# Attention and gated experts in one kernel: two of the first tile's eight units turned on TensorE instead of VectorE, and the second expert matrix loaded six steps later

## The chip, the cores and the metric

The kernel runs on one core of one Trainium2 chip. The core has five engines that each work through their own list of instructions in order: TensorE (PE, matrix products; its weight loads are shown as PEld), VectorE (DVE), ScalarE (ACT), GpSimd (POOL) and SyncE (SP, which here only issues transfers). Products land in PSUM, which has eight banks; everything else lives in SBUF. The metric is the device time of one execution in microseconds (us). Before the change it is 502.42 us, the median of three runs (501.6 to 503.89).

## The reference

```
attn_out = softmax(q @ k.T / 8) @ v            # 8 batches, 16 heads, 384 tokens, 64 wide; k and v shared by the heads
x        = attn_out with the heads side by side  # 3072 tokens x 1024
g_logits = x @ w_group                         # 4 groups, the largest wins
e_logits = x @ w_expert[g]                     # 4 experts in the group, the largest wins
out      = gate(g) * gate(e) * (relu(x @ w1[g, e]) @ w2[g, e])
```

All inputs are float32. Each token goes to one of 16 experts, and each expert is two 1024 x 1024 matrices.

## The kernel before, in words

A batch of 384 tokens is cut into three tiles of 128 tokens, so there are 24 tiles (t) of the eight batches (b). A tile's 16 heads make eight units (u) of two heads each. The kernel is written out as 96 steps (i, in the loop over `NSL`), two units to a step, four steps to a tile, twelve to a batch. The order of the work is written by hand: each engine runs what the source emits in the order in which it is emitted. `at(step, place, fn)` puts a piece of work at a place inside a step, and `run(step, place)` emits it there.

One unit passes through these stations.

- `scores` (L211): four products on PE into a two-bank PSUM tile `s`, of which there are two. The next step's unit can only start when ACT has finished with the bank pair that it takes over.
- `soft` (L228, L233): one maximum over both heads on DVE, then two exponentials on ACT, which also write the row sums. The result is `pr`.
- `norm` (L244, L248): a reciprocal of the sums on DVE, then a multiplication of each head's `pr` on POOL, four for the two units of a step. `norm` of step 0 is put off into step 1, at place "b", which lies between the first unit's exponentials and the second unit's maximum; all others stand at the end of their own step.
- `transp` (L254): two steps later DVE turns each 32 x 32 block of `pr` into `ring`, a buffer with three groups of four units. The blocks are turned, but not moved, so a key's place is split over partitions and columns.
- `pv` (L272): in the last two steps of the following tile, PE multiplies the eight units of a tile with the values, in 96 products. Each uses 32 keys, both halves of the array's columns (one per head) and 256 columns (eight units of 32 tokens). Four PSUM banks take the sums of the four groups of partitions.
- `pv_out` (L286, L287): four ACT copies into `xt`, and one POOL copy to bfloat16 into `xb`.

After the first tile of a batch, `logits` (L295) forms the gate's products from `xt` alone, in step 8 of the batch: 32 products with the gate's weights held in the array and 32 tokens streamed each. `logits_out` (L305) turns the result on DVE, and `gate_first`, `gate_choose`, `gate_score` and `gate_pick` choose the expert that most tokens of the tile want. `load_main` (L469) then loads that expert's two matrices over POOL's queue, two transfers to a matrix. In batch 0 the first matrix is put in step 9 and the second in step 11; in the other batches both are in step 9.

From step 17 of a batch on, `main_expert` runs the batch's rows through this expert in pieces between the attention's own work (`advance`): first 64 products with the first matrix (L494), then the products with the second (L510). A last part, after step 95, handles the tokens that this leaves out.

PSUM has six tiles in all: two of `s`, and four single banks from `xbank` that all other products share in turn. `busy` (L99) is a product with no use for its result; one stands in step 2, one in step 3, one in step 9. Queries of the first tiles are turned on PE (`q_group`, L189), two heads to a turn, and copied out by ACT (L193). Transfers of q, k and v go through SP's queue in order. `load_v` repeats the values on four groups of 32 partitions, so that group a can be used with any block of 32 keys.

Of the kernel before, what the change touches and what calls it, by code (L numbers as in the profile page):

```python
# [9 lines left out]
FP32 = mybir.dt.float32  # L10
BF16 = mybir.dt.bfloat16
I32 = mybir.dt.int32
P = 128
# [6 lines left out]
def kernel(  # L20
# [11 lines left out]
    nc = tc.nc  # L32
# [53 lines left out]
    st = {}  # L86
# [2 lines left out]
    NB = S // 32  # L89

    TQ = 5

    def xbank():
        x = ps_x.tile([P, 512], FP32, tag="x", name="x")
# [69 lines left out]
    def load_v(b):  # L164

        v_sb = qpool.tile([P, NB, D], FP32, tag="v")
        vv = v[b, 0].rearrange("(r n) d -> r (n d)", n=NB)
        for i in range(P // 32):
            nc.sync.dma_start(out=v_sb[32 * i:32 * (i + 1), :, :].rearrange("r n d -> r (n d)"), in_=vv)
        st["v", b] = v_sb  # L170

    def scale_k(b):
        kk = st["kk", b]
# [68 lines left out]
    def norm(us):  # L242
        rinv = ppool.tile([P, 2, 2], FP32, tag="rinv")
        nc.vector.reciprocal(out=rinv[:], in_=st.pop(("ssum", us[0]))[:])  # L244
        for k, u in enumerate(us):
            for h in range(2):
# [2 lines left out]
                    out=pr, in0=pr, scalar1=rinv[:, k, h:h + 1], scalar2=1.0, op0=ALU.mult, op1=ALU.mult  # L249
                )  # L250

    def transp(u):

        nc.vector.transpose(  # L254
            out=ring[:, (u // 4) % 3, u % 4].rearrange("p h s -> p (h s)"),
            in_=st.pop(("pr", u))[:].rearrange("p h s -> p (h s)"),
        )

    def pv(t, n0, n1):

        v_sb = st["v", t // ST]
        a, z = sorted(((2 * t) % 3, (2 * t + 1) % 3))
        if n0 == 0:
            st["o", t] = [xbank() for _ in range(P // 32)]
        o = st["o", t]

        turned = lambda n, h: n - n % ST + (n + 1) % ST if t < ST and h else n
        for n in range(n0, n1):
            for i in range(P // 32):
                r = slice(32 * i, 32 * (i + 1))  # L270
                for h in range(2):
                    nc.tensor.matmul(  # L272
                        out=o[i][h * D:(h + 1) * D, 0:2 * P].rearrange("d (g c q) -> d g c q", g=2, c=4),
                        lhsT=v_sb[r, turned(n, h), :], rhs=ring[r, a:z + 1:z - a, :, h, ts(n, 32)],
                        start=(n == 0), stop=(n == NB - 1), tile_position=(32 * i, h * D),
                    )

    def pv_out(t):
        b, j = t // ST, t % ST
        if j < 2:  # L280
            st["xt", b, j] = pool.tile([P, KO, ST - 1 if j else 1, P], FP32, tag=f"xt{j}", name="xt", bufs=1)
        xt = st["xt", b, min(j, 1)][:, :, max(j - 1, 0), :]
        if j == 0:
            st["xb", b] = pool.tile([P, KO, S], BF16, tag="xb", name="xb", bufs=2)
        for i, o in enumerate(st.pop(("o", t))):
            nc.scalar.copy(out=xt[:, :, ts(i, 32)], in_=o[:, 0:2 * P].rearrange("p (c q) -> p c q", c=KO))  # L286
        nc.gpsimd.tensor_copy(out=st["xb", b][:, :, ts(j, P)], in_=xt)  # L287

    def logits(b, j0, j1):

        xt = st.pop(("xt", b, j0))
        lt_ps = xbank()
        for ko in range(KO):
            for c in range(4):
                nc.tensor.matmul(  # L295
                    out=lt_ps[ts(c, 32), 0:32 * (j1 - j0)].rearrange("e (j q) -> e j q", q=32),
                    lhsT=wge[:, ko, :], rhs=xt[:, ko, :, ts(c, 32)],
                    start=(ko == 0), stop=(ko == KO - 1), tile_position=(0, c * 32),
                )
# [187 lines left out]
    def expert(xb, w1, w2, result, psum, on_act=None, split=False):  # L487
# [3 lines left out]
        for fc in range(FO):  # L491
# [9 lines left out]
            else:  # L501
                nc.vector.tensor_scalar(out=h_t[:, fc, :], in0=hp[:, 0:S], scalar1=0.0, scalar2=None, op0=ALU.max)
            yield
        for j in range(ST):
            widths = (512, 256, 256) if split and j == ST - 1 else (512, 512)
            at_ = 0
# [45 lines left out]
        st["alone"].append(rows)  # L552

    def main_expert(b, on_act):
        w1, w2 = st.pop(("w", b))

        def store(j, done, y):
            if b < B - 1:
# [12 lines left out]
                ))  # L571

        result = scaled(lambda: st["gsel", b][0], store)
        yield from expert(st["xb", b], w1, w2, result, any_bank, on_act, split=(b == B - 1))

    def few_ready():

# [177 lines left out]


    NSL = NU // 2
    SB = ST * 4
    NT = B * ST
    pending = []  # L760
# [22 lines left out]
    for b in range(B):  # L783
# [65 lines left out]
    q_group(0, 0, 0, 1)  # L849
    q_group(0, 0, 1, 2)  # L850
    at(0, "b", q_group, 0, 0, 2, 4)
    at(1, "b", norm, (0, 1))
    load_v(0)
    for i in range(NSL):
        t, p = i // 4, i % 4
# [171 lines left out]
```

## Time and profile before

| | before |
|---|---|
| median of three runs | 502.42 us |
| profiled execution | 502.84 us |
| its span, first to last instruction | 501.4 us |
| PE busy | 479.0 us |
| DVE busy | 412.7 us |
| ACT busy | 319.7 us |
| POOL busy | 292.4 us |

In the rows of the profile a name such as `pr<-s,nmx` gives the tile written and the tiles read; `x48` is a count; a number in square brackets is how long the engine had been idle before, and what released it. A row of the timeline joins neighbouring instructions of one kind: its second number runs from the start of the first to the end of the last. A float32 product appears as two rows of PE, so the 48 products of half a `pv` are "x96".

### The profile page before, as it was taken

The page shows a single profiled execution, that of the slowest core. Times are in us where ns is not written, and L with a number is a line of the kernel's source. Part 1 is how long each engine was busy: PE and PEld are TensorE (multiplying, and loading weights), DVE is VectorE, ACT ScalarE, POOL GpSimd, SP SyncE. Part 2 cuts the span into 40 slices and gives each one's busy share as a digit, 9 for nine tenths or more (in the row PEclk, how much of TensorE's full clock was granted, in tenths as well). Part 3 has the DMA queues.
Part 4 walks back from the last instruction along what each step waited for, and adds up shares of the span by engine and source line. Part 5 has one row for each costly group of instructions (what it writes and reads, how often), then busy time and mean ns, then how long its engine had stood idle before and what let it go on. Part 6 is the DMA issues. An engine that isn't in the chain of part 4 may idle for free. (4 is left out here: it accounts for less than half of the span.)

```text
span 501.4 us, 20025 instructions
## 1 busy us (share of the span) xinstructions
PE 479.0 (96%) x8251; PEld 257.4 (51%) x8251; DVE 412.7 (82%) x744; ACT 319.7 (64%) x999; POOL 292.4 (58%) x532
## 2 busy tenths in 40 slices
PE   7798789999999999999999999999999999999992
PEld 2254445545555455555555455554555455555651
DVE  4989979988899889898799988998799888892450
ACT  5776866667666775766765865766667666662420
POOL 2665955684576654585476654684566754765232
PEclk9999999999999999999999999999999999999998
DMA  7703995399946998379965999379974996059994
GB/s 109 166 5 63 209 241 144 76 173 233 258 78 126 217 244 225 75 135 228 243 138 92 200 237 255 79 136 225 221 187 78 194 238 170 3 97 220 250 219 147
DMA packets 63388, 83.17 MB, mean 166 GB/s; under 512 B 20151, under 2 KB 39739, under 8 KB 63040
## 3 DMA queue, kind: packets, MB, share of 16 engines
q0 software_dynamic: 18736, 39.32, 42.3%
q1 hardware_dynamic: 43472, 42.22, 34.5%
q8 instruction: 66, 1.08, 0.9%
q10 hardware_dynamic: 1088, 0.33, 0.3%
q14 instruction: 26, 0.21, 0.1%
HBM read 101.52 MB, written 18.22 MB: 239 GB/s over the span
## 5 line engine op out<-in xcount | busy, mean ns | idle before, releaser
L233 ACT ACTIVATE pr<-s,nmx 128x384 f32<-128x384 f32 x384 | 217.7, 579 | 130.9 <-DVE nmx L228 116.7
L248 POOL TENSOR_SCALAR pr<-pr,rinv 128x384 f32<-128x384 f32 x384 | 217.3, 585 | 142.7 <-DVE rinv L244 129.5
L228 DVE TENSOR_REDUCE nmx<-s 128x2 f32<-128x768 f32 (+1 forms) x193 | 174.5, 944 | 47.6 <-PE s L211 46.5
L254 DVE STREAM_TRANSPOSE ring<-pr 128x768 f32<-128x768 f32 x192 | 175.3, 951 | 0.1
L211 PE MATMUL s<-kt,qt 64*64 64x384 f32 x1536 | 148.8, 497 | 10.8 <-ACT pr L233 8.7
L272 PE MATMUL x<-ring,v_sb 32*64 32x256 f32 x4608 | 137.6, 379 | 0.0
L272 PEld LDWEIGHTS x<-ring,v_sb 32*64 32x64 f32 x4608 | 101.6, 131 | 42.7 <-issue 23.0
L211 PEld LDWEIGHTS s<-kt,qt 64*64 64x64 f32 x1536 | 48.1, 132 | 78.8 <-ACT pr L233 38.6
L233 ACT ACTIVATION_READ_ACCUMULATOR pr<-s,nmx 128x1 f32 x384 | 77.8, 203 | 0.0
L494 PE MATMUL x<-xb,w 128*128 128x384 bf16 x448 | 76.6, 327 | 0.0
L494 PEld LDWEIGHTS <-w 128*128 128x128 bf16 x512 | 47.6, 97 | 42.3 <-issue 12.6
L510 PE MATMUL x<-w,h_t 128*128 128x512 bf16 x288 | 65.3, 380 | 0.0
L510 PEld LDWEIGHTS <-h_t 128*128 128x128 bf16 x392 | 36.3, 97 | 51.3 <-issue 12.1
L469 POOL DMA_DIRECT2D w<-in_moe_w_dram x36 | 27.5, 771 | 12.2 <-issue 7.4
L286 ACT COPY xt<-x 128x256 f32<-128x256 f32 x96 | 28.8, 387 | 2.9 <-PE x L272 2.9
L500 ACT ACTIVATE h_t<-x 128x384 bf16<-128x384 f32 x56 | 25.4, 502 | 6.1 <-PE x L494 6.1
L287 POOL CAST xb<-xt 128x1024 bf16<-128x1024 f32 x24 | 24.9, 1036 | 4.5 <-ACT xt L286 4.5
L529 ACT ACTIVATE y<-x,gsel 128x512 f32<-128x512 f32 x36 | 24.9, 692 | 3.4 <-PE x L510 3.4
L200 DVE STREAM_TRANSPOSE qt<-q_sb 128x512 f32<-128x512 f32 x38 | 26.1, 687 | 0.0
L510 PE MATMUL sb<-w,h_t 128*128 128x512 bf16 (+1 forms) x104 | 21.8, 363 | 0.0
L529 ACT ACTIVATE y<-sb,gsel 128x512 f32<-128x512 f32 (+1 forms) x10 | 6.7, 666 | 17.6 <-PE sb L510 15.2
L295 PEld LDWEIGHTS x<-xt,wge 128*32 128x32 f32 x1024 | 12.9, 110 | 5.8 <-ACT y L529 2.5
(136 smaller groups left out, 160.9 us busy)
## 6 DMA issues: line engine op xcount, KB each, us to landing
w<-in_moe_w_dram POOLq DMA_DIRECT2D x36, 1024.0 KB, 17.1
q_sb<-in_q_dram SPq DMA_DIRECT2D x76, 224.0 KB, 6.2
out_dram<-y SPq DMA_DIRECT2D x84, 128.0 KB, 6.7
xb_scratch<-xb SPq DMA_DIRECT2D x7, 768.0 KB, 4.3
v_sb<-in_v_dram SPq DMA_DIRECT2D x32, 96.0 KB, 3.6
kk<-in_k_dram SPq DMA_DIRECT2D x28, 92.0 KB, 3.5
q_sb<-in_q_dram SPq DMA_DIRECT2D x16, 128.0 KB, 3.4
q_sb<-in_q_dram ACTq DMA_DIRECT2D x2, 96.0 KB, 3.2
```

The costliest lines, as they stand in the source:

```text
L200: nc.vector.transpose(out=qt[:].rearrange("p (x d) -> p x d", d=32), in_=q_sb[:, :, 0:32])
L211: nc.tensor.matmul(out=s[m * D:(m + 1) * D, h, 0:S], lhsT=qt[r, ts(2 * cc + m, D)], rhs=kt[r, :], start=True, stop=True, tile_position=(h ...
L228: top = nc.vector.tensor_reduce(out=nmx[:, hs], in_=s[:, hs, 0:S], axis=AX.X, op=ALU.max, negate=True)
L233: ex = nc.scalar.activation(out=pr[:, h, :], in_=s[:, h, 0:S], func=ACTF.Exp, bias=nmx[:, h:h + 1], scale=1.0, accum_out=ssum[:, k, h:h + 1],)
L248: nc.gpsimd.tensor_scalar(out=pr, in0=pr, scalar1=rinv[:, k, h:h + 1], scalar2=1.0, op0=ALU.mult, op1=ALU.mult)
L254: nc.vector.transpose(out=ring[:, (u // 4) % 3, u % 4].rearrange("p h s -> p (h s)"), in_=st.pop(("pr", u))[:].rearrange("p h s -> p (h s)"),)
L272: nc.tensor.matmul(out=o[i][h * D:(h + 1) * D, 0:2 * P].rearrange("d (g c q) -> d g c q", g=2, c=4), lhsT=v_sb[r, turned(n, h), :], rhs=ri ...
L286: nc.scalar.copy(out=xt[:, :, ts(i, 32)], in_=o[:, 0:2 * P].rearrange("p (c q) -> p c q", c=KO))
L469: nc.gpsimd.dma_start(out=w[:, o:o + 4, :], in_=views[n][ds(e, 1), :, o:o + 4, :].rearrange("o p c f -> (o p) c f"))
L494: nc.tensor.matmul(out=hp[:, 0:S], lhsT=w1[:, ko, ts(fc, P)], rhs=xb[:, ko, :], start=(ko == 0), stop=(ko == KO - 1))
L510: nc.tensor.matmul(out=yp, lhsT=h_t[:, fo, ts(j, P)], rhs=w2[:, fo, at_:at_ + w], start=(fo == 0), stop=(fo == FO - 1),)
L529: nc.scalar.activation(out=y[:, at_:at_ + w], in_=yp, func=ACTF.Copy, scale=g)
```

## The change

Two of tile 0's eight units, units 1 and 3 (`WHOLE`), no longer go through `transp`. `whole` turns each of their heads on PE, three 128 x 128 turns into one bank, and ACT copies the bank into two places of `ring` that the first tile leaves free. These two units stand in steps 2 and 3, in place of the two products of `busy`.

A whole turn puts 128 keys on the partitions in one piece, so these units need the values in another layout. `v_whole` builds it in step 2 with twelve small POOL copies inside SBUF, into the space of `grem_all`, which is written for good only in step 18. `pv_whole` (steps 4 and 5) multiplies each of the two units with it, six products of 128 columns, into one bank, and `whole_out` (step 5) copies the result into `xt`.

The first tile's `pv` then has six units instead of eight: as many products as before, each over 192 columns instead of 256. Its `xt` holds the units in another order (0, 2, 4, 5, 6, 7, 1, 3), and the POOL copy to `xb` restores the right one in three pieces.

The gate's products of batch 0's first tile hold the tokens in the array and stream the gate's 32 columns: 8 products instead of 32, with the result already lying by tokens, so that `logits_out` becomes a plain DVE copy.

`norm` of steps 0, 2 and 3 (`LATE`) is put off into the following step's place "b"; before, only that of step 0 was. The second matrix of batch 0 is loaded in step 17 instead of step 11, and `expert` asks for it only when its second half begins. `scale_k` of batch 1 moves from step 7 to step 6. No other batch is touched.

```diff
+    WHOLE = (1, 3)
+    PARTS = [u for u in range(8) if u not in WHOLE]
+    order = PARTS + list(WHOLE)
+    slot_of = {u: x for x, u in enumerate(PARTS)}
...
+    def v_whole():
+        vw = grem_all[:].rearrange("p e j -> p (e j)").rearrange("p (h m d) -> p h m d", h=2, d=D)
+        for a in range(4):
+            r = slice(32 * a, 32 * (a + 1))
+            for h in range(2):
+                n = [keys(4 * m + a, h) for m in range(ST)]
+                for m0, m1 in ((0, ST),) if h == 0 else ((0, 2), (2, ST)):
...
+                    nc.gpsimd.tensor_copy(out=vw[r, h, m0:m1, :], in_=st["v", 0][r, n[m0]:end:step, :])
...
+    def whole(u):
+        pr = st.pop(("pr", u))
+        prt = ring[:, 1, 2 + WHOLE.index(u)]
+        for h in range(2):
+            pt = xbank()
+            for m in range(ST):
+                nc.tensor.transpose(out=pt[:, ts(m, P)], in_=pr[:, h, ts(m, P)], identity=ident[:])
+            nc.scalar.copy(out=prt[:, h, :], in_=pt[:, 0:S])
+
+    def pv_whole(u):
...
+        for m in range(ST):
+            for h in range(2):
+                nc.tensor.matmul(
+                    out=st["ow"][h * D:(h + 1) * D, ts(k, P)], lhsT=st["vw"][:, h, m, :],
+                    rhs=ring[:, 1, 2 + k, h, ts(m, P)], start=(m == 0), stop=(m == ST - 1), tile_position=(0, h * D),
+                )
...
     def transp(u):
+        if u in slot_of:
+            nc.vector.transpose(
+                out=ring[:, slot_of[u] // 4, slot_of[u] % 4].rearrange("p h s -> p (h s)"),
...
+            return
+        if u in WHOLE:
+            return
...
+        nc_ = len(PARTS) if t == 0 else 8
...
+                    to = o[i][h * D:(h + 1) * D, 0:32 * nc_]
...
+            if b == 0 and j0 == 0:
+                nc.tensor.matmul(
+                    out=lt_ps[:, 0:32], lhsT=xt[:, ko, 0, :], rhs=wge[:, order[ko], :],
+                    start=(ko == 0), stop=(ko == KO - 1),
+                )
+                continue
...
-        nc.vector.transpose(
+        (nc.vector.tensor_copy if b == 0 and j0 == 0 else nc.vector.transpose)(
...
+    LATE = (0, 2, 3)
...
-            at(s0 + (9 if b else 11), "g", load_main, b, 1)
+            at(s0 + (9 if b else 17), "g", load_main, b, 1)
...
-            at(s0 + 7, "g", scale_k, b + 1)
+            at(s0 + (7 if b else 6), "g", scale_k, b + 1)
...
-    for x, where in ((2, "m2"), (3, "m2"), (9, "m3")):
-        at(x, where, busy, ident)
+    for x, u in enumerate(WHOLE):
+        at(2 + x, "m2", whole, u)
+        at(4 + x, "m2", pv_whole, u)
+    at(5, "e", whole_out)
+    at(2, "g", v_whole)
+    at(9, "m3", busy, ident)
...
-        if i:
+        if i in LATE:
+            at(i + 1, "b", norm, us)
+        else:
             norm(us)
```

More of the change, by code (lines that the diff above doesn't have):

```diff
@@ L170, in load_v @@
         st["v", b] = v_sb
+    def v_whole():
[5 more added lines that the diff above has]
+                for m0, m1 in ((0, ST),) if h == 0 else ((0, 2), (2, ST)):
+                    step = n[m0 + 1] - n[m0] if m1 - m0 > 1 else 1
+                    end = n[m1 - 1] + (1 if step > 0 else -1)
+                    nc.gpsimd.tensor_copy(out=vw[r, h, m0:m1, :], in_=st["v", 0][r, n[m0]:end:step, :])
+        st["vw"] = vw
     def scale_k(b):
@@ L250, in norm, with keys, whole_out, first_xt @@
                 )
-    def transp(u):
+    def keys(n, h):
+        return n - n % ST + (n + 1) % ST if h else n
+    def whole(u):
[7 more added lines that the diff above has]
+    def pv_whole(u):
+        k = WHOLE.index(u)
+        if k == 0:
+            st["ow"] = xbank()
+        for m in range(ST):
[4 more added lines that the diff above has]
+                )
+    def whole_out():
+        nc.scalar.copy(
+            out=first_xt()[:, len(PARTS):KO, :], in_=st.pop("ow")[:, 0:2 * P].rearrange("p (c q) -> p c q", c=2)
+        )
+    def first_xt():
+        if ("xt", 0, 0) not in st:
+            st["xt", 0, 0] = pool.tile([P, KO, 1, P], FP32, tag="xt0", name="xt", bufs=1)
+        return st["xt", 0, 0][:, :, 0, :]
+    def transp(u):
+        if u in slot_of:
+            nc.vector.transpose(
+                out=ring[:, slot_of[u] // 4, slot_of[u] % 4].rearrange("p h s -> p (h s)"),
+                in_=st.pop(("pr", u))[:].rearrange("p h s -> p (h s)"),
+            )
+            return
+        if u in WHOLE:
+            return
         nc.vector.transpose(
@@ L285, in pv_out @@
         for i, o in enumerate(st.pop(("o", t))):
-            nc.scalar.copy(out=xt[:, :, ts(i, 32)], in_=o[:, 0:2 * P].rearrange("p (c q) -> p c q", c=KO))
-        nc.gpsimd.tensor_copy(out=st["xb", b][:, :, ts(j, P)], in_=xt)
+            nc.scalar.copy(
+                out=xt[:, 0:nc_, ts(i, 32)], in_=o[:, 0:32 * nc_].rearrange("p (c q) -> p c q", c=nc_)
+            )
+        if t == 0:
+            for at0, at1 in ((0, 2), (2, 6), (6, 8)):
+                c0, c1 = order[at0], order[at0 + 1]
+                nc.gpsimd.tensor_copy(
+                    out=st["xb", b][:, c0:order[at1 - 1] + 1:c1 - c0, ts(j, P)], in_=xt[:, at0:at1, :]
+                )
+        else:
+            nc.gpsimd.tensor_copy(out=st["xb", b][:, :, ts(j, P)], in_=xt)
     def logits(b, j0, j1):
```

24 lines of the change are left out of this document (17 added, 7 removed).

## The prediction

> **What bounds the kernel now.** I read the page's busy shares first, then a table of stretches, then the timeline of the first 110 us, where all edits lie. The first fence has the page's shares and the stretches, whose columns are the stretch, its length, the busy time of PE, PEld, DVE, ACT and POOL with counts, the granted clock, the DMA share and GB/s.
>
> ```profile
> PE 479.0 (96%) x8251; PEld 257.4 (51%) x8251; DVE 412.7 (82%) x744; ACT 319.7 (64%) x999; POOL 292.4 (58%) x532
> ...
> 15.00:20.00 5.00, 3.75 (x30) 0.98 (x32) 5.00 (x8) 3.63 (x14) 2.65 (x5) 1.00 1.05 205
> 20.00:25.00 5.00, 3.74 (x32) 1.40 (x32) 5.00 (x9) 3.25 (x10) 3.53 (x7) 1.00 0.50 104
> 30.00:35.00 5.00, 5.00 (x140) 3.00 (x128) 4.18 (x6) 2.89 (x11) 2.26 (x4) 1.00 0.02 7
> ...
> 56.00:74.00 18.00, 15.14 (x336) 8.11 (x336) 15.29 (x24) 12.35 (x41) 11.79 (x20) 1.00 1.11 223
> 81.00:98.00 17.00, 17.00 (x325) 9.58 (x313) 15.89 (x32) 11.88 (x39) 9.60 (x19) 1.00 0.36 70
> ...
> 100.00:400.00 300.00, 300.00 (x5266) 161.16 (x5251) 264.62 (x443) 203.83 (x644) 185.18 (x322) 1.00 0.83 178
> ```
>
> From some 75 us on PE never rests, and nothing edited there is PE work. Before that DVE is full (15 to 25 us) or PE (30 to 35 us). So whatever an edit saves or costs before 75 us moves all that follows by the same amount, and the question is what each early step gains.
>
> **Steps 2 to 5: DVE, and behind it a loop.** The timeline gives start, duration, engine and line.
>
> ```profile
> 12.95 1.83 DVE L228 TENSOR_REDUCE nmx<-s 128x2 f32<-128x768 f32 x2
> 14.69 1.83 DVE L254 STREAM_TRANSPOSE ring<-pr 128x768 f32<-128x768 f32 x2
> 15.04 0.58 ACT L233 ACTIVATE pr<-s,nmx 128x384 f32<-128x384 f32 x1
> 16.06 0.21 ACT L233 ACTIVATION_READ_ACCUMULATOR pr<-s,nmx 128x1 f32 x1
> 16.32 0.88 PE L211 MATMUL s<-kt,qt 64*64 64x384 f32 x8 [0.25 <-ACT pr L233]
> 16.44 0.14 DVE L244 RECIPROCAL rinv<-ssum 128x4 f32<-128x4 f32 x1
> 16.50 1.79 DVE L228 TENSOR_REDUCE nmx<-s 128x2 f32<-128x768 f32 x2
> 27.08 1.81 DVE L228 TENSOR_REDUCE nmx<-s 128x2 f32<-128x768 f32 x2
> ```
>
> A maximum takes 0.87 us of DVE (two from 12.95 to 14.69), a turn 0.875 (14.69 to 16.44), a reciprocal 0.06 until the next starts (16.44 to 16.50). Two, two and one make 3.55 per step; the first maxima of steps 2 and 6 stand at 12.95 and 27.08, 14.13 apart, which is four such steps.
>
> Take a turn away, and another limit is near. A unit's two exponentials hold its `s` for 1.23 us (15.04 to 16.27), its successor's scores start 0.05 later and take 0.88, the maximum starts 0.06 after that and needs 0.96, the exponential starts 0.03 later: 3.21 us per step, whatever DVE has to do. So two turns (1.75 us) can't be won whole.
>
> I now go through the new order with these durations. Step 2: two maxima and one turn, 2.6 us of DVE, so the loop decides: step 3's first maximum at 16.14 instead of 16.50. Step 3 has 2.7 us of DVE, so the loop again: step 4's first maximum at 19.35. Step 4 has two turns and two reciprocals (3's was put off into it); its second maximum waits for the second unit's loop until 20.48, then 0.87 + 1.75 + 0.06 lead to 23.16. Step 5 is unchanged, 3.55: step 6 begins at 26.71 instead of 27.08. **Gain 0.37 us.** What is late next is the ACT-to-scores loop, not DVE.
>
> **What this leans on.** POOL, PE and ACT must keep up in these steps.
>
> ```profile
> 10.46 1.97 SPq L169 DMA_DIRECT2D v_sb<-in_v_dram  x4
> DMA to landing us min/median/max: 2.5/2.9/3.1
> 13.13 2.26 POOL L248 TENSOR_SCALAR pr<-pr,rinv 128x384 f32<-128x384 f32 x4 [0.25 <-DVE rinv L244]
> L436 POOL TENSOR_TENSOR gw<-wt 128x12 f32<-128x12 f32 x8 | 1.7, 208 | 6.8 <-DVE wt L433 6.8
> L603 POOL CAST c<-ident 128x128 bf16<-128x128 f32 x1 | 0.3, 293 | 0.0
> L248 POOL TENSOR_SCALAR pr<-pr,rinv 128x384 f32<-128x384 f32 x384 | 217.3, 585 | 142.7 <-DVE rinv L244 129.5 <-DVE es L431 13.0
> 6.89 0.87 PE L189 MATMUL x<-ident,q_sb 128*128 128x128 f32 x6
> 13.68 1.13 PE L99 MATMUL x<-ident 128*128 128x512 f32 x2
> ```
>
> `v_whole`: twelve copies of 64 to 192 columns. No such copy is in the trace; the nearest rows are 208 ns (12 columns), 293 ns (128) and 585 ns (384), so the twelve cost 2.5 to 7.0 us; I take 0.29 each, 3.5 us, since 128 columns is their mean. The values have landed before 15.6 (last issue before 12.43, at most 3.1 more). The copies stand behind `norm` of step 1 (until 15.39) and end near 18.9; behind them `norm` of step 2 ends at 21.2. Its first unit is then ready at 20.05 and the second at 21.2; DVE asks for them at 21.35 and 22.2. Cost nothing, but with little to spare: at 0.585 each the copies end at 22.4, the first turn waits until 23.5 and the second until 24.7 instead of 22.2, and up to 2.5 us are lost.
>
> `whole`: six turns take 0.87 us, where `busy` took 1.13; PE waits for ACT there, so nothing. Its two ACT copies stand between the exponentials of one step and the next, in the 1.25 us that ACT spent waiting there; two of 384 columns take some 0.8. `pv_whole` (two times 12 rows) lies in PE's waits in steps 4 and 5, and `whole_out`, one more copy of 256 columns, in ACT's wait in step 5. All four cost nothing while the loop's 3.21 stands; without that cover each would cost its 0.4 to 0.9 once.
>
> **Steps 6 and 7: PE.**
>
> ```profile
> 27.80 2.85 PE L272 MATMUL x<-ring,v_sb 32*64 32x256 f32 x96
> 30.57 1.52 PE L211 MATMUL s<-kt,qt 64*64 64x384 f32 x16
> 31.52 1.82 DVE L228 TENSOR_REDUCE nmx<-s 128x2 f32<-128x768 f32 x2 [0.82 <-PE s L211]
> 32.02 2.85 PE L272 MATMUL x<-ring,v_sb 32*64 32x256 f32 x96
> 35.74 1.82 DVE L228 TENSOR_REDUCE nmx<-s 128x2 f32<-128x768 f32 x2 [0.60 <-PE s L211]
> 36.84 0.76 PE L295 MATMUL x<-xt,wge 128*32 128x32 f32 x64
> 38.08 0.88 PE L211 MATMUL s<-kt,qt 64*64 64x384 f32 x8 [0.48 <-ACT pr L233]
> 39.90 1.78 DVE L228 TENSOR_REDUCE nmx<-s 128x2 f32<-128x768 f32 x2
> ```
>
> The next scores queue behind `pv`, and DVE waits for them, 0.82 and 0.60 us. The 96 rows follow each other at 26 ns; streaming 192 columns instead of 256 would make it 19.6 ns, and a half 2.2 us, 0.65 less. The ends are 0 (the rows don't stream-bind) and 0.65 to 0.7 (DVE's own chain, 34.05 against 35.74, allows no more). I take 0.65 and 0.63: that rows can follow faster shows in the gate's products, 64 rows of 32 columns in 0.76 us. **Gain 1.28 us.**
>
> **Step 8, the gate.** Eight products with the tokens held. Each of its 16 rows loads 128 x 128 in float32; the turns do that at 0.105 us a row (0.87 for six), which makes up to 1.9 us against 0.76. PE has 0.48 to spare before the next scores, and their maximum at 39.90 starts 0.94 after the scores end at 38.96. 1.2 us more just fits under 1.36. Cost nothing; between a gain of nothing and a loss of 0.3. The DVE copy in place of a turn of 32 columns, three POOL copies for one, and `scale_k` a step earlier on a POOL that is 58% busy: nothing, POOL's rows lie two steps ahead of their use.
>
> **The second matrix.**
>
> ```profile
> 55.94 1.55 POOL L469 DMA_DIRECT2D w<-in_moe_w_dram  x2
> 65.49 0.88 PE L211 MATMUL s<-kt,qt 64*64 64x384 f32 x8 [1.15 <-DVE nmx L228]
> 82.95 2.26 POOL L248 TENSOR_SCALAR pr<-pr,rinv 128x384 f32<-128x384 f32 x4 [1.95 <-DVE es L431]
> 106.98 3.63 PE L510 MATMUL x<-w,h_t 128*128 128x512 bf16 x16
> ```
>
> Its two issues leave POOL at 55.94 and come back in the 1.95 us that POOL waits ahead of 82.95: nothing. The transfer took 18 us there (55.94 to 74, DMA share 1.11) and moves to some 81 to 98, where the share is 0.36. SP's loads of queries, issued shortly before and behind it, will take longer; the matrix is first used at 106.98, so it has 8 us to spare. At 65.49 a unit's scores came 1.15 us late, although `s` was free; the weight loads there name "issue". It is the only gap of that kind in the run, and lies in the stretch that the second matrix fills. Ends: nothing, and 1.15 gained. The trace doesn't show the cause, and 98 to 128 us is as full without such a gap, so I take the middle, **0.6 us.**
>
> **Sum.** 0.37 + 1.28 + 0.6 = 2.25 us off the profiled execution's 502.84, which is its span of 501.4 and 1.4 around it: 500.6. The median shown lies 0.42 lower, so 500.2 against 502.42.
>
> **The rivals.**
> - *Narrower products are no shorter.* Then 0.37 + 0.6: 501.4. For it: a half's weight loads span almost as long as its products. Against it: the gate's 64 rows in 0.76 us. The Trainium skill, "TensorE: Matmul & The Clock Gate", section "Wait — 56ns, not 53.3ns?", gives a floor of about 25 ns from one small product to the next, "however small N is"; by that a half would fall by only 0.1. The gate's rows, 12 ns apart, disagree, though each product makes two of them.
> - *GpSimd is late.* At 0.585 us per copy `v_whole` loses 2.5 and leaves 2.25 - 2.5: 502.7. Against it: POOL's small rows near 0.29.
> - *TensorE's clock falls, and the kernel is slower.* `busy` goes from steps 2 and 3. These rows, with PE's busy time, clock, DMA share and GB/s, show that the clock can halve.
>
> ```profile
> 18.81:22.33 3.52, 2.34 (x20) 1.00 0.28 61
> 492.00:494.00 2.00, 0.47 (x20) 1.00 0.74 285
> 498.00:500.00 2.00, 0.00 (x0) 0.50 0.01 4
> ```
>
> At half speed scores last 0.88 longer in each of steps 2 to 5 and each half of `pv` 2.2: 3.5 + 4.4 more, some 508. It decides if the clock falls for as little as 3 us. Against it: 18.81 to 22.33 has no `busy`, PE is two thirds full there, and the clock is 1.00; it fell only some 4 us after all PE work had ended. The Trainium skill, same page, "Part 4: PE-mode transpose", says that transposes don't count as PE-busy "the same way", which speaks for this rival; the two steps from 18.81 to 25.9, with turns and scores alone, don't bear it out.
> - *The gap at 65.49 stays, or another comes where the matrix now loads:* 0.6 to 1.7 less, 500.8 to 501.9.
>
> **How the numbers follow.** Forecast 0.47, with its own range 499.3 to 500.9; products no shorter 0.20; the gap stays or moves 0.16; GpSimd late 0.11; clock 0.06. The best sum, with all of the gap, is 2.8 off 502.42: 499.6, less 0.4 for the scatter of medians. The upper end takes in the late copies, 502.7. So 499.2 to 502.8. One measurement of this kernel tells about 0.5%, 2.5 us, from no change: the forecast lies just inside. Faster by more (under 499.9) 0.40, mostly the forecast with all of the gap; within 0.45; slower 0.15, the clock and late copies together with a moved gap.
>
> **What would show it.** Step 6's first maximum near 26.7, step 8's near 34.1 (from the profile's start); a half of the first `pv` at 2.2 us; twelve copies near 0.29 on POOL; PE's clock 1.00 throughout; no wait of DVE for POOL at its turns in step 4; no gap before scores between 60 and 100 us. Wrong if the first `pv` keeps 2.85, if turns in step 4 wait for `norm`, or if the loop takes more than 3.3 us per step.

## The result and the profile after

| | before | after |
|---|---|---|
| median of 17 runs each | 502.23 us | 500.77 us |
| range of these runs | 500.96 to 505.87 | 498.84 to 502.46 |
| span of the profiled execution | 501.4 us | 498.9 us |

The ratio is 0.9959, with a 95% interval of 0.9941 to 0.9976. The medians lie 1.46 us apart, and the interval allows 1.2 to 3.0. With another 12 runs of the changed kernel the ratio was 0.9967 (0.9948 to 0.9986). So the gain is real, some 0.3 to 0.4%, and smaller than the half per cent that the prediction counted as a difference.

The page's shares after, and of the stretches that the prediction showed of before these:

```profile
PE 479.3 (96%) x8218; PEld 262.1 (53%) x8235; DVE 411.5 (82%) x742; ACT 321.0 (64%) x1004; POOL 295.6 (59%) x546
...
15.00:20.00 5.00, 3.79 (x34) 1.47 (x38) 4.12 (x6) 4.82 (x18) 4.76 (x16) 1.00 1.12 214
...
56.00:74.00 18.00, 16.30 (x342) 9.08 (x342) 16.41 (x28) 13.80 (x47) 11.41 (x21) 1.00 0.63 153
81.00:98.00 17.00, 17.00 (x345) 10.19 (x345) 16.14 (x30) 12.03 (x40) 11.53 (x23) 1.00 0.90 173
100.00:400.00 300.00, 299.42 (x5193) 162.29 (x5191) 264.19 (x442) 204.45 (x646) 182.21 (x318) 1.00 0.84 179
```

From 15 to 20 us DVE is no longer full (4.12 of 5), ACT almost is (4.82), and POOL went from 2.65 to 4.76. The granted clock is 1.00 in every stretch. The second matrix's transfer left 56 to 74 us (DMA share 1.11 before, 0.63 now) and came to 81 to 98 (0.36, now 0.90). In the last row PE is 0.58 us short of full, where before it was full. These are eleven pieces of 0.05 us; a second profile of the same code, with 17 more records of PE, has none of them, so they are records that this one lacks and not rests.

The timeline of the first 40 us and of step 15, after:

```profile
15.37 3.17 POOL L185 COPY grem_all<-v_sb 32x192 f32<-32x192 f32 x12
16.18 0.96 DVE L244 TENSOR_REDUCE nmx<-s 128x2 f32<-128x768 f32 x1 [0.48 <-PE s L227]
19.47 0.96 DVE L244 TENSOR_REDUCE nmx<-s 128x2 f32<-128x768 f32 x1 [0.32 <-PE s L227]
21.46 1.83 DVE L304 STREAM_TRANSPOSE ring<-pr 128x768 f32<-128x768 f32 x2
26.78 1.82 DVE L244 TENSOR_REDUCE nmx<-s 128x2 f32<-128x768 f32 x2
27.50 2.21 PE L335 MATMUL x<-ring,v_sb 32*64 32x192 f32 x96
34.17 1.82 DVE L244 TENSOR_REDUCE nmx<-s 128x2 f32<-128x768 f32 x2
35.35 1.87 PE L371 MATMUL x<-wge,xt 128*128 128x32 f32 x16
...
61.87 1.52 PE L227 MATMUL s<-kt,qt 64*64 64x384 f32 x16
63.32 2.85 PE L335 MATMUL x<-ring,v_sb 32*64 32x256 f32 x96
```

The maxima at 16.18 and 19.47 now wait for PE's scores: DVE has time to spare. The first half of `pv` takes 2.21 us. The maximum of step 8 starts at 34.17, where it started at 35.74. In step 15 the two units' scores run in one row of 16, 1.52 us, and `pv` follows at once; the pause of 1.15 us between the two units' scores at 65.49 is gone.

In what follows, a step's start is the start of the first `nmx` row on DVE that belongs to it (16.18, 19.47, 26.78 and 34.17 above are steps 3, 4, 6 and 8), and its length is the distance to the next step's start. Steps of one kind have the same length in most places (4.22 or 4.23 us for the ones with half a `pv`), so a longer one stands out. Worked out this way, after minus before:

| start of step | 3 | 4 | 6 | 7 | 8 | 15 | 16 | 48 | 60 | 72 | 95 |
|---|---|---|---|---|---|---|---|---|---|---|---|
| us | -0.32 | -0.54 | -0.30 | -0.93 | -1.57 | -1.59 | -2.97 | -3.48 | -2.78 | -2.20 | -2.11 |

So 1.57 us is won by step 8, another 1.38 in step 15 (5.61 to 4.23 us long), and some 0.5 more by step 48. Then 1.4 us is lost, in steps that no edit touches: step 55 is 4.83 instead of 4.23, step 63 is 4.47, step 67 is 4.56. This is what the prediction did not have, and what most of the experiments are about.

### The profile page after: what moved, and what is told of

It is laid out like the page before. It is cut to its first block, busy times and chain, and to the rows that moved or that the text cites. A ratio compares the mean times of both kernels' runs of the same rounds, so it can differ in the third digit from the quotient of the medians.

```text
span 498.9 us, 19995 instructions
## 1 busy us (share of the span) xinstructions
PE 479.3 (96%) x8218; PEld 262.1 (53%) x8235; DVE 411.5 (82%) x742; ACT 321.0 (64%) x1004; POOL 295.6 (59%) x546
## 5 line engine op out<-in xcount | busy, mean ns | idle before, releaser
L311 DVE STREAM_TRANSPOSE ring<-pr 128x768 f32<-128x768 f32 x184 | 168.1, 952 | 0.1
L335 PE MATMUL x<-ring,v_sb 32*64 32x256 f32 (+1 forms) x4608 | 137.2, 376 | 0.1
L335 PEld LDWEIGHTS x<-ring,v_sb 32*64 32x64 f32 x4608 | 103.0, 131 | 41.1 <-issue 23.1
L353 ACT COPY xt<-x 128x256 f32<-128x256 f32 (+1 forms) x96 | 28.6, 386 | 2.5 <-PE x L335 2.5
L363 POOL CAST xb<-xt 128x1024 bf16<-128x1024 f32 x23 | 23.8, 1036 | 4.5 <-ACT xt L353 4.5
L429 POOL TENSOR_TENSOR mask_all<-oh 128x48 bf16<-128x48 f32 x8 | 2.1, 269 | 22.4 <-DVE oh L425 22.4
```

The lines of the kernel that those rows point to most:

```text
L311: nc.vector.transpose(out=ring[:, (u // 4) % 3, u % 4].rearrange("p h s -> p (h s)"), in_=st.pop(("pr", u))[:].rearrange("p h s -> p (h s)"),)
L335: nc.tensor.matmul(out=to.rearrange("d (c q) -> d c q", c=nc_) if t == 0 else to.rearrange("d (g c q) -> d g c q", g=2, c=4), lhsT=v_sb[r, ...
L353: nc.scalar.copy(out=xt[:, 0:nc_, ts(i, 32)], in_=o[:, 0:32 * nc_].rearrange("p (c q) -> p c q", c=nc_))
```

## The experiments

Each is the changed kernel with one edit, unless another is named. Where no number of runs is given, the time is that of one execution, and the kernel before stood at 502.18 to 502.32 us beside it. Single executions of one kernel scatter by some 2 us either way, once by 3.6 (the two ranges above), so these experiments are read by the lengths of their steps, not by their totals.

### The transfer of the second matrix, put back or moved alone

```diff
-            at(s0 + (9 if b else 17), "g", load_main, b, 1)
+            at(s0 + (9 if b else 11), "g", load_main, b, 1)
```

> The changed kernel, with the second matrix loaded in step 11 again. Theory A (the transfer of the second matrix made the gap of step 15): step 15 is 5.4 to 5.6 us long again, and everything behind it 1.2 to 1.4 us later than in the changed kernel. Theory B (the gap hangs on where the blocks of PE's instruction list end, and the change has moved these ends by some 32 instructions): step 15 stays at 4.2 us.

The kernel before with only this line the other way round, and the second matrix asked for when it is first used:

> The kernel before, with the second matrix in step 17 and nothing else. PE's list of instructions is the same as before. Theory A: step 15 falls from 5.6 to 4.2 us. Theory B: step 15 stays at 5.2 to 5.6 us, since the block ends at the same place.

Measured: 502.38 us with the transfer put back, 500.95 us with the transfer moved alone. The first starts 1.5 us late (its step 2 starts at 14.49 instead of 12.98, which no edit explains). Step 15 is 4.26 and 4.24 us long, so the gap is gone in both. PE's timeline with the transfer put back:

```profile
69.70 0.52 PE L377 MATMUL x<-xt,wge 128*32 128x64 f32 x18
71.22 0.87 PE L377 MATMUL x<-xt,wge 128*32 128x64 f32 x46 [1.00 <-issue]
```

The gap has moved into step 16, between two of the gate's products, with no releaser but "issue". So each theory is borne out by one run and missed by the other. The gap at 65.49 went with the transfer, but the transfer doesn't say where a gap falls; nor does a gap in step 15 need it, since two kernels below, the one without turns and the one with 192 more instructions, load the second matrix in step 17 too, and their step 15 is 5.76 us long. What differs ahead of step 15 between the kernel before and this one is the number of PE's instructions: the first tile's edits take some 32 away by step 8.

The DMA view shows what comes late. Packets, megabytes and share of the engines by queue, from 60.5 to 62.5 and from 62.5 to 64.5 us, first in the kernel before, then with the transfer moved alone:

```profile
q0 software_dynamic: 178, 0.36, 95.7%
q1 hardware_dynamic: 79, 0.07, 13.3%
...
q0 software_dynamic: 153, 0.31, 82.8%
q1 hardware_dynamic: 153, 0.14, 26.4%
q8 instruction: 1, 0.02, 2.9%
```

and

```profile
q1 hardware_dynamic: 476, 0.40, 110.6%
q8 instruction: 1, 0.02, 4.2%
...
q1 hardware_dynamic: 309, 0.44, 108.7%
```

q8 is the queue that loads instructions: 66 packets of some 16 KB in a run. These two kernels have the same PE list up to there. With the matrix (q0) on the engines, the packet comes only in the later stretch, and the gap at 65.49 opens behind it.

### Sixteen products without a use at PE's start

`busy` behind the first one gets sixteen more products of 16 columns, whose results are not used. The trace counts two PE instructions for each, 32 in all.

```diff
+        for _ in range(more):
+            nc.tensor.matmul(out=x[:, 0:16], lhsT=a[:], rhs=a[:, 0:16], start=True, stop=True)
...
-    busy(ones)
+    busy(ones, 16)
```

> The changed kernel with 16 tiny products more (32 PE instructions) behind the very first product, where PE waits for the first transfer of k. Theory B: the blocks end at the places of the kernel before, so the long steps are those of before (15, 31 and 43) and not those of the changed kernel (43, 55, 63 and 67); up to step 14 nothing changes by more than 0.1 us. Theory A: the steps' lengths stay those of the changed kernel.

Measured: 499.97 us. The steps begin 0.28 us later (step 2 at 13.26 instead of 12.98), and yet the last one starts 0.75 us earlier than in the changed kernel (443.64 against 444.39). Step 43 is 4.23 us long instead of 4.56, step 63 4.23 instead of 4.47, step 67 4.23 instead of 4.56; step 79 is longer (4.45 against 4.28), and step 55 stays long (4.60 against 4.83). Neither theory has this list right: steps 15 and 31, which were to be long again, are 4.26 and 4.23. How much of it is the padding's own shows in the second profiles further down. Steps 43 and 79 are alike in both profiles of the changed kernel (4.56 and 4.57; 4.28 and 4.23) and in both versions padded by 32 (4.23 and 4.23; 4.45 and 4.45). Steps 55, 63 and 67 are 4.28, 4.23 and 4.23 in the changed kernel's second profile, with nothing added. So 32 more instructions at the start move what is lost in these two steps, 180 and 350 us later; the other three can be the one execution.

### The whole turns taken out

`WHOLE` is empty and the two `busy` are back; the put-off `norm`, the gate by tokens and the late second matrix stay.

```diff
-    WHOLE = (1, 3)
+    WHOLE = ()
...
-    for x, u in enumerate(WHOLE):
...
-    at(2, "g", v_whole)
-    at(9, "m3", busy, ident)
+    for x, where in ((2, "m2"), (3, "m2"), (9, "m3")):
+        at(x, where, busy, ident)
```

> The changed kernel with no unit turned whole: all eight go through VectorE, the first product has 256 columns again, the two products of busy are back; the late norm of steps 0, 2 and 3, the gate by tokens and the late second matrix stay. My working: steps 2 to 5 take 3.5 us each and steps 6 and 7 4.4 and 4.2, so the first maximum of step 8 stands at 35.5 to 35.8, as before. Rival: the late norm alone wins a part, then at 35.3 or less.

Measured: 518.77 us, 18 us above the changed kernel. Up to step 8 all goes as in the kernel before: steps 2 to 5 last 3.49, 3.51, 3.57 and 3.51 us, steps 6 and 7 4.45 and 4.23, and step 8's maximum starts within 0.03 of the old 35.74:

```profile
35.77 1.82 DVE L244 TENSOR_REDUCE nmx<-s 128x2 f32<-128x768 f32 x2 [0.60 <-PE s L227]
```

So the 1.57 us of steps 2 to 7 hang on the turns; the put-off reciprocals alone bring nothing. The other 16 us come later, in steps that no edit here touches: step 11 lasts 5.52 us (4.44 in the changed kernel), 12 4.50 (3.68), 15 5.76 (4.23), 31 6.12 (4.23), 55 6.39 (4.83), 79 6.04 (4.28), 87 5.27 (4.24), and 40, 52, 64 and 88 last 6.87 to 6.91 (6.04). The rows of PE's timeline in steps 11, 15 and 40, the stretch behind the first of them, and the page's group of `pv`:

```profile
56.17 2.84 PE L227 MATMUL s<-kt,qt 64*64 64x384 f32 x16 [2.22 <-ACT pr L249]
66.83 1.52 PE L335 MATMUL x<-ring,v_sb 32*64 32x256 f32 x39
69.24 1.96 PE L335 MATMUL x<-ring,v_sb 32*64 32x256 f32 x57 [0.90 <-issue]
193.12 0.41 PE L377 MATMUL x<-xt,wge 128*32 128x64 f32 x11 [0.58 <-issue]
...
56.20:59.00 2.80, 2.80 (x17) 0.78 (x17) 2.80 (x5) 1.52 (x5) 2.59 (x5) 0.50 1.12 208
...
L335 PE MATMUL x<-ring,v_sb 32*64 32x256 f32 x4608 | 143.8, 379 | 7.0 <-issue 6.8
```

The changed kernel's row for the same group:

```profile
L335 PE MATMUL x<-ring,v_sb 32*64 32x256 f32 (+1 forms) x4608 | 137.2, 376 | 0.1
```

There are two mechanisms. In step 11 PE rests for 2.22 us, since DVE's turn waits 1.65 us for `norm`, which POOL begins 2.35 us later than in the kernel before, behind the issue of the first matrix; why that issue comes later was not followed. Behind the rest PE's clock is 0.50 for 2.8 us, and 16 rows of scores take 2.84 us instead of 1.52. Steps 11 and 12 lose 1.9 us, and the rest alone does it: the next kernel has them at 5.49 and 4.51 us with the clock at 1.00. The other 14 go mostly in `pv` and the gate: half a `pv` breaks in two, 39 rows and 57, with nothing of the kernel's own that the second part waited for, and the gate's 64 rows break into 53 and 11. `pv` is 6.6 us longer busy (1.3 of them are the first tile's wider products), and idle for 6.9 us more.

This kernel with 32 of the useless products at the start (64 instructions):

> The kernel without whole units again, with 32 tiny products more (64 PE instructions) behind the first product, so that the blocks of PE's instruction list end about where they do in the changed kernel. Theory B (the place of the block ends makes the long steps): the long steps of 4.5 to 6.9 us go, and the time falls from 518.8 to 501 to 503 us, that of the kernel before. Rival (without whole units something else slows every batch): it stays above 512 us.

Measured: 506.48 us, 12.3 less with 64 instructions more, though its step 8 starts later (35.94). It is more than the 501 to 503 expected. Steps 40, 52, 64 and 88 are back at 6.04 us, 15 at 4.43, 79 at 4.23. Steps 11 and 12 stay long (5.49 and 4.51), and step 14 is now 6.06 instead of 4.43: there PE rests 1.92 us for ACT, and the clock is 0.50 from 63 to 66 us. Behind the rest of step 11, 2.19 us, it stays at 1.00:

```profile
56.30 0.88 PE L229 MATMUL s<-kt,qt 64*64 64x384 f32 x8 [2.19 <-ACT pr L251]
...
56.30:59.70 3.40, 2.34 (x20) 0.84 (x20) 3.40 (x6) 1.73 (x6) 3.19 (x6) 1.00 1.12 210
62.60:66.00 3.40, 3.40 (x68) 2.06 (x72) 3.11 (x5) 2.36 (x8) 2.03 (x5) 0.50 1.18 213
```

So most of the 18 us was neither the turns nor anything else that these edits do. It was how many instructions PE's list holds ahead of those places.

### The changed kernel with more of the useless products

96 products (192 instructions), and 32 (64 instructions):

> The changed kernel with 96 tiny products more (192 PE instructions, 64 short of a block), so that the blocks end about where they do in the kernel without whole units. Theory B: steps 15, 31, 55 and 79 grow beyond 5 us and steps 40, 52, 64 and 88 to 6.9 us, and the time is 508 to 520 us. Rival (the place of the block ends is worth a microsecond or two at most): 499 to 504 us.

> The changed kernel with 32 tiny products more (64 PE instructions). Theory B gives no size without a measured phase; if 32 instructions took the long steps away, 64 may bring others: 498 to 503 us. Rival: like the changed kernel, 499 to 501.5 us.

Measured: 515.48 and 502.26 us. At step 8 they are 2.20 and 0.49 us late (36.37 and 34.66). With 192, steps 40, 52, 64, 76 and 88 last 6.84 to 6.90 us, step 15 5.76, 43 5.30, 51 5.05, 79 5.54; steps 31 and 55, expected beyond 5 us too, are 4.75 and 4.23. By step 95 (458.51 against 444.39) 11.9 us are lost beyond the delay at the start. With 64, step 14 lasts 5.37 (4.44), 26 4.71 (4.23), and by step 95 (446.32) 1.4 us is lost beyond the delay. From 0 to 32, 64 and 192 instructions the time goes 500.8, 500.0, 502.3, 515.5; a cost of the products themselves would rise with their number and stand at the start.

### The small copies twice

Each of `v_whole`'s twelve copies is made two times.

```diff
-                    nc.gpsimd.tensor_copy(out=vw[r, h, m0:m1, :], in_=st["v", 0][r, n[m0]:end:step, :])
+                    for _ in range(2):
+                        nc.gpsimd.tensor_copy(out=vw[r, h, m0:m1, :], in_=st["v", 0][r, n[m0]:end:step, :])
```

> The changed kernel with each of GpSimd's twelve copies of the values made twice; PE's list is unchanged. My working: the copies take 6.3 instead of 3.2 us and end at 21.7, norm of step 2 ends at 24.0, and step 4's first turn waits until 22.9 and its second until 24.0 instead of 22.3: step 5's first maximum some 1.7 us later, and that stays to the end. Rival (the copies have room): no change above 0.2 us.

Measured: 505.35 us. The timeline of POOL, DVE and PE, and two stretches:

```profile
15.19 7.36 POOL L186 COPY grem_all<-v_sb 32x192 f32<-32x192 f32 x24
23.82 2.10 DVE L305 STREAM_TRANSPOSE ring<-pr 128x768 f32<-128x768 f32 x2 [2.46 <-POOL pr L265]
28.20 2.84 PE L228 MATMUL s<-kt,qt 64*64 64x384 f32 x16 [2.33 <-ACT pr L250]
37.92 1.82 DVE L245 TENSOR_REDUCE nmx<-s 128x2 f32<-128x768 f32 x2
...
25.90:28.20 2.30, 0.00 (x1) 0.00 (x1) 2.30 (x5) 1.29 (x5) 2.30 (x5) 1.00 0.00 0
28.20:31.00 2.80, 2.80 (x21) 0.78 (x22) 2.24 (x4) 1.94 (x7) 2.60 (x6) 0.51 0.01 3
```

The copies take 4.2 us more, and step 8 starts 3.9 us later (37.92 against 34.17, and this run began 0.18 earlier). DVE waits 2.46 us for the normalized unit at its first turn of step 4 (23.82 instead of 21.46); steps 4, 5 and 6 last 6.62, 3.93 and 4.51 us instead of 3.80, 3.51 and 3.80. The wait for POOL is the one expected, but its price was set too low: step 5 starts 2.8 us later instead of 1.7, since the second set of copies takes 4.2 us and not 3.1. Behind the wait PE has nothing to do from 25.90 to 28.20, and when the scores come the clock is 0.51 and they take 2.84 us instead of 1.52, and the `pv` behind them begins at a clock below 1.00 too. Steps 5 and 6 lose the other 1.1 us.

### The reciprocals of steps 2 and 3 at their old place

```diff
-    LATE = (0, 2, 3)
+    LATE = (0,)
```

> The changed kernel with the reciprocals of steps 2 and 3 back at the end of their own steps; only step 0's is late. Theory (the loop from ACT to the scores sets steps 2 and 3, and the late reciprocal keeps DVE out of it): each reciprocal now waits for ACT's last sum ahead of the next first maximum, so steps 2 and 3 last some 3.3 to 3.5 us instead of 3.19 and 3.29, and step 8's first maximum comes 0.3 to 0.5 later. Rival (the late reciprocals do nothing, all of the gain comes from the turns): the same first maxima within 0.1.

Measured, DVE's timeline of steps 2 to 4:

```profile
13.34 1.83 DVE L244 TENSOR_REDUCE nmx<-s 128x2 f32<-128x768 f32 x2
...
16.69 0.18 DVE L260 RECIPROCAL rinv<-ssum 128x4 f32<-128x4 f32 x1 [0.64 <-ACT pr L249]
16.78 1.83 DVE L244 TENSOR_REDUCE nmx<-s 128x2 f32<-128x768 f32 x2
...
20.22 0.18 DVE L260 RECIPROCAL rinv<-ssum 128x4 f32<-128x4 f32 x1 [0.72 <-ACT pr L249]
...
27.52 1.82 DVE L244 TENSOR_REDUCE nmx<-s 128x2 f32<-128x768 f32 x2
```

DVE stands idle for 0.64 and 0.72 us, since the reciprocal waits for ACT's last sum and the next maximum queues behind it. Steps 2 and 3 last 3.45 and 3.53 us instead of 3.19 and 3.29. From step 2 to step 6 it is 14.18 us (27.52 - 13.34), where the changed kernel takes 13.80 (26.78 - 12.98), the kernel before 14.13 and the one without turns 14.08. So in these steps the turns alone bring nothing, the put-off reciprocals alone next to nothing, and both together 0.33 us. The total, 499.68 us, is still below the changed kernel's: its last step starts at 444.11, since steps 55, 63 and 67 last 4.56, 4.26 and 4.23 us instead of 4.83, 4.47 and 4.56 (4.28, 4.23 and 4.23 in the changed kernel's second profile).

### On one chip: a padded version, the changed kernel again, the transfer alone

The padded version has the sixteen useless products in step 2, ahead of unit 1's turns, where PE waits for ACT.

```diff
             pt = xbank()
+            for _ in range(16 if u == 1 and h == 0 else 0):
+                nc.tensor.matmul(out=pt[:, S:S + 16], lhsT=ones[:], rhs=ones[:, 0:16], start=True, stop=True)
             for m in range(ST):
```

> The changed kernel with sixteen tiny bfloat16 products (32 more instructions of PE, results unused) ahead of unit 3's turns in step 3, where PE waits for ACT anyway; the version at PE's start cost 0.28 us there. Theory (where the blocks of PE's instruction list end decides the later steps): the block ends fall as in the version padded by 32, so steps 31 and 43 near 4.23, step 55 near 4.6, the first maximum of step 8 within 0.1 of the changed kernel's, and about 0.3 to 0.8 us less than the changed kernel in all. Rival (the padding helped by its place at the start, by delaying PE): no gain, step 55 as in the changed kernel, 4.8.

> The changed kernel itself, for a comparison on the same chip with the padded one: 500.8 us, 0.9960 of before.

> The kernel before with only the second matrix moved, timed in rounds. One look gave 500.95 us. If that holds, this one line brings 1.2 to 1.5 us, as much as all edits together (500.8), since what the first tile wins in steps 2 to 8 is lost again later to other ends of PE's instruction blocks. If the look was a lucky one, 501.4 to 501.8, which is the gap of 1.15 us less what the moved transfer costs elsewhere.

(The first text names step 3 and unit 3; it is step 2 and unit 1.) Measured in 12 runs each, against 29 of the kernel before at 502.18 us:

| kernel | median, us | ratio to before (95%) |
|---|---|---|
| changed kernel, padded by 32 instructions | 499.50 | 0.9955 (0.9940 to 0.9970) |
| changed kernel | 500.82 | 0.9967 (0.9948 to 0.9986) |
| before, only the second matrix moved | 501.35 | 0.9978 (0.9962 to 0.9995) |

In the padded version the products cost nothing: from step 2 to step 8 it is 21.20 us (34.64 - 13.44), in the changed kernel 21.19. The later steps are not those of the version padded at the start: 43 is 4.23 as expected, but 55 is 4.23 instead of 4.6, 31 is 4.39, and 19 is 4.76. So the place of the padding matters too, or the one execution does. It has the lowest median of the three, but the means of its runs and of the changed kernel's (499.74 and 500.63) are 0.9 us apart, with an interval of about 0.9 either way. It is not settled that it is better. Of the transfer moved alone, 0.8 us remain of the 1.4 that its first execution had; its profile here begins late (step 2 at 14.36), as that of the transfer put back did, and its step 15 is 4.23 us long.

The changed kernel's second profile shows the point of all this best, since there the code is the same to the last instruction. Step 31 lasts 5.81 us, against 4.23 in the first profile. PE's timeline, then the DMA view from 136 to 138 and from 138 to 139.8 us; first the first profile:

```profile
138.26 2.85 PE L335 MATMUL x<-ring,v_sb 32*64 32x256 f32 x96
...
q1 hardware_dynamic: 495, 0.42, 110.2%
q8 instruction: 1, 0.02, 3.2%
...
q1 hardware_dynamic: 314, 0.26, 84.9%
```

and the second:

```profile
138.33 1.52 PE L335 MATMUL x<-ring,v_sb 32*64 32x256 f32 x39
140.80 1.96 PE L335 MATMUL x<-ring,v_sb 32*64 32x256 f32 x57 [0.95 <-issue]
...
q1 hardware_dynamic: 478, 0.41, 116.2%
...
q1 hardware_dynamic: 299, 0.24, 78.1%
q8 instruction: 1, 0.02, 4.9%
```

PE is in the same place at the same time in both (138.26 and 138.33). SP's loads of values and queries (q1) fill the DMA engines in both. In the first the instruction packet comes before 138, and `pv` runs through; in the second it comes after 138, and `pv` breaks behind its 39th row until 140.80.

How general this is shows when the packets of the traces are set against PE's list one by one. Nine of the fourteen traces hold every record of PE. In these nine, all 15 rests of PE between 60 and 470 us that last 0.15 us or more and have no releaser stand a multiple of 256 instructions apart in PE's list, its waits counted (one instruction off, once): behind 1,729 in step 15 of the kernel without turns, behind 1,985 in step 16 of the one with the transfer put back, behind 4,545 in step 31 both of the second profile above and of the kernel without turns. From step 15 on, 36 steps of the nine are more than 0.15 us longer than the median of the same step over all traces. Each of the 36 holds the first instruction of such a block of 256, and that instruction starts 1.2 to 1.65 us after the end of the packet that carries its block. No block of the nine traces starts sooner behind its packet, and half of them start 4 us or more behind it. So in the long steps PE had run through one block before the next had come.

How late a packet comes goes with the other transfers. In the kernel before, where nothing else is on the DMA engines, it starts 0.3 to 1.5 us after PE has entered the block ahead of it. Ahead of the gap at 65.49, with a DMA share of 1.11, it started 6.5 us after; with the second matrix moved alone, still 4.9 and 4.6 in the two profiles. In step 31 of the changed kernel it started 1.6 us after in the first profile and 3.5 in the second.

## Why the prediction was right, and where it was not

Forecast was 500.2 us with 499.2 to 502.8; the medians are 500.77 and 500.82, within half a per cent of before, and that case had the largest chance (0.45). The sum behind it was 2.25 us, of which the medians show 1.46 and 1.36. Its terms one by one:

- *Steps 2 to 5, 0.37.* Right: 0.33 (14.13 to 13.80 us; by the working's own terms step 3 starts at 16.16, not 16.14, and the gain is 0.35). The loop from ACT to the scores decides, as the waits for PE at 16.18 and 19.47 show. It takes 3.19 and 3.29 us, not 3.21 and 3.21, and step 5 starts at 23.27, not 23.16. The working used the put-off reciprocals without saying that the gain hangs on them; with them at their old place nothing of it is left.
- *Steps 6 and 7, 1.28.* Right: 1.27 (1.57 by step 8, less 0.30). A half of `pv` takes 2.21 us, as worked out from 19.6 ns a row. The rival by which narrower products are no shorter is out: the Trainium skill's floor of about 25 ns ("TensorE: Matmul & The Clock Gate", section "Wait — 56ns, not 53.3ns?") would have left it near 2.75.
- *The gate, nothing.* Right: 16 rows take 1.87 us, and the gain at step 15 is the 1.59 that it was near step 8.
- *POOL, nothing.* Right, with the twelve copies at 3.17 us instead of 3.5 and `norm` ending in time for the turn at 21.46. The rival's price was too low. It said at most 2.5 us lost with copies of 7.0 us; with 7.36 us 2.8 were lost by step 5, and 3.9 by step 8, as the clock fell behind the wait.
- *The clock.* It stayed at 1.00, though the two `busy` were replaced by turns. That rival is out for this kernel. Its mechanism is real, though, and nearer than the text had it: not some 4 us after the end of all work, but behind a rest of 2.2 us (step 11 without the turns) or 2.3 us (with the copies twice) the clock was halved for some 3 us. The length of the rest alone does not decide it: behind 2.19 us, in the kernel without turns padded by 64 instructions, it stayed at 1.00.
- *The second matrix, 0.6, the middle of nothing and 1.15.* Mis-sized: step 15 became 1.38 us shorter, so all of the gap went. The rival that it moves is half true: with the transfer left where it was, the gap came up at 71.22 instead.
- *"Whatever an edit saves or costs before 75 us moves all that follows by the same amount."* This is the step that failed. 2.97 us stood at step 16, 3.48 at step 48, and 2.11 at step 95; in the second profile 1.6 us went in step 31 alone. The argument was that PE never rests after 75 us and that nothing edited there is PE work. But the edits changed the length of PE's instruction list, and with it, and with small shifts in time against the loads, which products stand at the end of what has been fetched when the next packet is late. The gap at 65.49 was not the only one of its kind, as the prediction has it: the profile of before holds two more places, steps 31 and 43, which are 4.58 and 4.86 us long instead of 4.23. PE counts as busy there, but half a `pv` of step 43 takes 3.48 us instead of 2.85:

```profile
198.75 3.48 PE L272 MATMUL x<-ring,v_sb 32*64 32x256 f32 x96
```

So two errors lie behind the 0.6 us between forecast and median, and they pull against each other: 0.8 us more was won at step 15 than the sum had, and of the 2.97 us that stood at step 16 0.9 were lost by step 95 (in the second profile 1.4 of 2.85). That the forecast came this near is in part luck.

What is shown is that gaps without a releaser come and go with the number of instructions ahead of them (64 and 192 added, with nothing else changed; for 32 added, in two steps on which four profiles agree), and that the long steps from step 15 on stand where an instruction packet came late (36 of 36 in nine traces). That the transfers on the DMA engines make it late is shown by the packets' times, and by one load taken away: without the second matrix the packet ahead of step 15 came sooner and the gap at 65.49 went. The big differences, 12 us and more, rest on one execution of each kernel, but they agree with each other by the places of their long steps. Not shown is why the loads stood otherwise against the same packet in two executions of the same code.

## What to carry to other kernels

In a long unrolled kernel whose TensorE list streams small products, a gain of a few microseconds early on can shrink or grow by the mere number of instructions ahead of the places where loads fill the DMA engines; so compare the lengths of equal steps over the whole run before crediting an edit, take a second profile of the same code (here one step differed by 1.6 us between two), and look for products that break in two with no releaser but "issue". A few useless products in an engine's idle time are a cheap way to move this, though it is not settled that they gained anything here, and a way to test whether a difference is the edit's own. Where two limits lie within a few tenths of each other, as DVE and the loop through ACT do here, edits can be worth something only together, so undo them one at a time.

## What the runs showed of the hardware that was not expected

The number of PE instructions ahead changed the same kernel's time by up to 14.7 us (500.8 to 515.5 with 192 more), and in another by 12.3 us (518.8 to 506.5 with 64 more). In the trace, the instruction queue's row is this, the same in the changed kernel and in the one of 518.8 us:

```profile
q8 instruction: 66, 1.08, 0.9%
```

That is 16.4 KB a packet, and the changed kernel's 16,453 rows of PE and PEld make some 250 rows a packet; with PE's waits counted it is the 256 found above. The Trainium skill, "Runtime: NRT & Kernel Launch", section "Instruction fetch mechanics", says that an engine's instructions come in blocks of 16 KiB, 256 instructions, which agrees. It also says that crossing a block's end is "mostly hidden". In most steps that holds here too; in the kernel of 518.8 us it does not, where `pv` alone waited 6.8 us for "issue". From the end of a packet to the first instruction of its block it took at least 1.2 us.

The clock can fall for a short rest of PE. In the kernel before, the rest of 1.15 us at 65.49 left it at 1.00; behind rests of 2.22 and 2.33 us it was 0.50 and 0.51, each for some 3 us, and the scores took 1.3 us longer. Behind one of 2.19 us it stayed at 1.00, so something besides the length decides, and no run here shows what. The Trainium skill, "TensorE: Matmul & The Clock Gate", section "HAM oscillation — how this bites in real kernels", warns of idle gaps of more than about 3.4 us; here shorter ones did it.

Small POOL copies take 230 ns for 64 columns and 340 for 192, so some 175 ns at any length and 0.86 ns for each column:

```profile
L185 POOL COPY grem_all<-v_sb 32x192 f32<-32x192 f32 x4 | 1.4, 340 | 0.1
L185 POOL COPY grem_all<-v_sb 32x64 f32<-32x64 f32 x4 | 0.9, 230 | 0.0
```
